# Dynamic convolution, layer norm and feed-forward on one core: the softmax by logarithms into two small PSUM tiles, another opening and another order of all engines

## The chip, the cores and the metric

The kernel runs on one core of one Trainium2 chip. The metric is device microseconds of one execution; before the change the median of three timed runs is 874.82 us (874.36 to 877.87). PE is TensorE, DVE is VectorE, ACT is ScalarE, POOL is GpSimd, and SP is the engine that issues most transfers.

## The reference

Inputs are x (8 x 4224 x 192, f32), weight_gen (8 x 4224 x 8 heads x 7), a layer-norm gain and two weights in f64 (192 x 768 and 768 x 192).

```python
w = softmax(weight_gen, axis=-1)                 # 7 taps, 1e-9 added to the sum
y[b, s, h*24+g] = sum_k w[b, s, h, k] * x_pad[b, s+k, h*24+g]   # 6 zero rows ahead
xn = (y - mean) / sqrt(var + 1e-6) * g_ln        # over the 192 columns
out = y + relu(xn @ w_ch1) @ w_ch2
```

## The kernel before, in words

The 33792 rows are laid out as 128 partitions x 264 columns of rows. A column holds one row of 192 values on every partition. Columns are taken in parts (`PARTS`: six of 4, six of 8, fifteen of 12, then 8 and 4) for the norm, in softmax pieces (`SOFT`: 4, 8, then 12 each) and in chunks of 4 or 6 columns for the convolution. x lies in a ring of 36 columns.

Softmax of a piece (L419 to L465): DVE takes the maximum (L434), POOL subtracts it (L436), ACT takes exp (L439), DVE sums (L443), ACT forms 1/sum as exp(-ln) (L446, L447), DVE refines it by three small instructions (L453 to L455), and DVE multiplies (L459) into one PSUM tile `wn` of two banks, which holds a whole piece.

Convolution of a chunk (L470 to L540): four DVE products (L505), `c0`, `c1`, `c3` with two taps each and `c2` with one tap into `y`; POOL issues two adding transfers (`d0`, `d1`, L511) and does four additions (`a0` to `a3`, L508). A part's norm (L548 to L647): ACT sums and squares row by row (L558, L563), a root by ln and exp (L586 to L588), five small DVE instructions (L591 to L597, "newton"), then for each group of 4 columns ACT scales (L609, `xh`) and rounds to f16 (L629, `hi`), POOL forms the low half (L642, `lo`), and SP issues a transposing transfer (L646, `turn`).

The feed-forward of a group has three units on PE (L664, 36 f16 products each, two row halves side by side) into one of two PSUM tiles `ph`; after each, ACT evicts with relu (L679) and DVE forms the low half (L681). The output is made in two halves, `p0` and `p1` (L715, 72 products each); the halves swap PSUM banks, so `p1` waits for an empty marker instruction, `hop`, that waits for `p0`; before the change the marker stands on SP (L725). DVE adds y (L767, `f`) and SP stores. The order on PE is unit, unit, p0 of the group before, unit, p1. 66 groups follow one another; the last output is L744.

The weights come as f64 and are rebuilt from their words in the opening (`from_double`, L810): ACT squares, four DVE steps put the words together, ACT sums squares; PE adds over partitions (L854), which gives a scale; ACT makes the high f16 half of W1 (L896), POOL the low one (L899), SP swaps partition halves (L903). W2 follows in the same manner (L919 to L933). Eleven products of 512 columns (L636, "wake") run on PE ahead of the first unit.

Every operation has a number in the table `PLACE`; operations are issued in the order of these numbers, so the table is the order on every engine. Engines take their own instructions strictly in that order. A `turn` and an adding transfer are also kept apart: each waits for the last of the other kind ahead of it.

Of the kernel before, what the change touches and what calls it, by code (L numbers as in the profile page):

```python
# [16 lines left out]
P = 128  # L17
ALPHA = 8.0
NT = 4

PARTS = (4,) * 6 + (8,) * 6 + (12,) * 15 + (8, 4)
SOFT = (4, 8) + (12,) * 21
DIRECT = 0
CHUNK = 6
RING = 36
# [6 lines left out]
    'wload': (0, 1, 30, 25, 35, 80, 81, 249, 257, 427, 634, 489, 783, 994, 748, 993, 1166, 1074, 1355, 1499,  # L32
        1370, 1571, 1769),
    'load': (6, 5, 33, 37, 36, 78, 79, 178, 183, 177, 256, 191, 340, 248, 303, 381, 426, 341, 568, 608, 564,
        713, 681, 682, 750, 780, 861, 953, 998, 1109, 997, 1176, 1157, 1235, 1263, 1368, 1289, 1460, 1531, 1572,
        1656, 1637, 1702, 1673, 1720, 1789, 1858, 1894, 1953, 2010, 2084, 2085),
    'w_load': (38, 24, 23, 7, 9, 10),
    'w_load2': (39,),
    'w_as': (82,),
    'w_av': (60, 62, 70, 89),  # L40
    'w_an': (100,),
    'w_cs': (102,),
    'w_cv': (26, 32, 48, 103),
    'w_cn': (105,),
    'w_s1': (120, 121, 123, 131, 139),
    'w_h': (154, 155, 145, 146),
    'w_l': (184, 152),
    'w_m': (189, 190, 182, 181),
    'w_c2s': (106, 122, 156),
    'w_c2v': (71, 85, 87, 115, 126, 128, 130, 132, 141, 143, 158, 161),  # L50
# [4 lines left out]
    'sub': (3, 8, 44, 51, 111, 237, 321, 432, 550, 665, 852, 758, 956, 1145, 1041, 1266, 1339, 1473, 1559, 1678,
        1757, 1855, 1970),
    'exp': (11, 16, 45, 52, 135, 277, 322, 440, 551, 666, 856, 802, 965, 1169, 1051, 1283, 1340, 1476, 1561,
        1695, 1784, 1869, 2005),
    'sum': (12, 17, 49, 53, 159, 279, 352, 456, 558, 687, 876, 832, 974, 1187, 1066, 1395, 1393, 1509, 1593,
        1716, 1802, 1875, 2024),  # L60
    'rcp': (13, 18, 54, 55, 160, 299, 437, 464, 640, 728, 882, 902, 986, 1192, 1172, 1399, 1446, 1510, 1594,
        1751, 1803, 1882, 2032),
# [34 lines left out]
    'sums': (64, 66, 95, 96, 136, 134, 170, 171, 239, 231, 247, 276, 318, 298, 320, 330, 395, 368, 392, 394,  # L97
# [163 lines left out]
def kernel(  # L261
# [735 lines left out]
```

## Time and profile before

| what | us |
|---|---|
| median of three timed runs | 874.82 |
| span of the profiled execution | 871.6 |
| PE, DVE, POOL, ACT busy | 793.9, 778.0, 697.6, 679.1 |
| first unit on PE starts | 67.02 |
| last product on PE ends | 867.26 |

The profiled execution's time is given by its span, from the first to the last instruction; the timed runs hold 3.2 us more around it. Busy is the time in which an engine worked; the two row halves of a unit run side by side, so a PE that is busy all the time is not yet a proof of a bound, which is why the chain and the gaps between products are read as well.

### The profile page before, as it was taken

The page shows a single profiled execution, that of the slowest core. Times are in us where ns is not written, and L with a number is a line of the kernel's source. Part 1 is how long each engine was busy: PE and PEld are TensorE (multiplying, and loading weights), DVE is VectorE, ACT ScalarE, POOL GpSimd, SP SyncE. Part 2 cuts the span into 40 slices and gives each one's busy share as a digit, 9 for nine tenths or more (in the row PEclk, how much of TensorE's full clock was granted, in tenths as well). Part 3 has the DMA queues.
Part 4 walks back from the last instruction along what each step waited for, and adds up shares of the span by engine and source line. Part 5 has one row for each costly group of instructions (what it writes and reads, how often), then busy time and mean ns, then how long its engine had stood idle before and what let it go on. Part 6 is the DMA issues. An engine that isn't in the chain of part 4 may idle for free.

```text
span 871.6 us, 37255 instructions
## 1 busy us (share of the span) xinstructions
PE 793.9 (91%) x16581; PEld 785.1 (90%) x16581; DVE 778.0 (89%) x799; ACT 679.1 (78%) x1776; POOL 697.6 (80%) x405
## 2 busy tenths in 40 slices
PE   0028999999999999999899999999999999999998
PEld 0016999999999999999899999999999999999997
DVE  6999999999999999999889999999999998974442
ACT  1798888888788898789598878787898888685741
POOL 4999999999789898897887988779888887857100
PEclk9999999999999999999999999999999999999999
DMA  8958878798897789789796798877988848643262
GB/s 210 270 119 182 181 161 179 143 190 191 185 199 149 169 183 216 137 179 180 152 212 142 156 210 163 164 200 178 182 167 157 205 111 196 117 84 77 44 178 56
DMA packets 138328, 143.23 MB, mean 164 GB/s; under 512 B 107575, under 2 KB 109111, under 8 KB 138167
## 3 DMA queue, kind: packets, MB, share of 16 engines
q1 hardware_dynamic: 123175, 88.95, 44.2%
q0 software_dynamic: 14688, 51.91, 31.0%
q8 instruction: 129, 2.11, 1.0%
q14 instruction: 32, 0.26, 0.1%
q10 hardware_dynamic: 304, 0.00, 0.0%
HBM read 36.43 MB, written 25.95 MB: 72 GB/s over the span
## 4 chain that ended last, share of the span: by engine, by line
PE 64%; ACT 1%; DVE 1%; issue 1%; DVEq 0%; ACTq 0%
PE po L715 32%; PE ph L664 32%; PE ph L744 1%; ACT junk L563 1%; DVE pr L505 1%; DVE hlo L681 0%; ACT junk L558 0%; ACT hh L679 0%; DVE y L767 0%; ACT s L586 0%; ACT rr L447 0%; ACT rr L446 0%; ACT s L587 0%; DVE wn L593 0%; DVE wn L595 0%
## 5 line engine op out<-in xcount | busy, mean ns | idle before, releaser
L508 POOL TENSOR_TENSOR y<-y,pr 128x1152 f32<-128x1152 f32 (+1 forms) x204 | 503.1, 2488 | 27.6 <-DMA pr<-pr 14.1
L664 PE MATMUL ph<-xT,c_w 64*128 64x256 f16 x7128 | 416.0, 270 | 8.9 <-DVE hlo L681 8.1
L664 PEld LDWEIGHTS <-c_w 64*128 64x128 f16 x7128 | 386.5, 94 | 14.0 <-issue 12.7
L715 PE MATMUL po<-c_w2h,hh 64*128 64x192 f16 x3120 | 388.1, 243 | 2.6 <-issue 2.5
L715 PE MATMUL po<-c_w2h,hlo 64*128 64x192 f16 x3120 | 388.1, 243 | 1.4 <-issue 1.4
L715 PE MATMUL po<-c_w2l,hh 64*128 64x192 f16 x3120 | 388.0, 243 | 0.5 <-issue 0.5
L505 DVE TENSOR_TENSOR pr<-x,wn 128x2304 f32<-128x2304 f32 (+1 forms) x153 | 337.2, 2214 | 3.8 <-DMA x<-in_x_dram 2.7
L715 PEld LDWEIGHTS <-hh 64*128 64x128 f16 x6240 | 309.4, 94 | 3.7 <-issue 3.7
L681 DVE SCALAR_TENSOR_TENSOR hlo<-ph,hh 128x1024 f16<-128x1024 f32 x198 | 238.6, 1217 | 52.3 <-ACT hh L679 52.0
L679 ACT ACTIVATE hh<-ph 128x1024 f16<-128x1024 f32 x198 | 199.5, 1014 | 108.0 <-PE ph L664 104.9
L715 PEld LDWEIGHTS <-hlo 64*128 64x128 f16 x3120 | 177.3, 94 | 1.5 <-issue 1.5
L642 POOL TENSOR_TENSOR hl<-xh,hl 128x768 f16<-128x768 f32 x66 | 113.8, 1758 | 52.1 <-ACT hl L629 52.1
L511 POOL DMA_DIRECT2D pr<-pr x102 | 102.2, 1110 | 53.7 <-DMA xT<-hl 33.2
L609 ACT ACTIVATE xh<-y,s 128x192 f32<-128x192 f32 x264 | 124.4, 535 | 18.7 <-DVE s L597 18.2
L563 ACT ACTIVATE junk<-y,s 128x192 f32<-128x192 f32 x264 | 119.6, 453 | 6.8
L558 ACT ACTIVATE junk<-y 128x192 f32<-128x192 f32 x264 | 95.0, 360 | 17.7 <-POOL y L508 11.6
L767 DVE SCALAR_TENSOR_TENSOR y<-po,c_fs,y 128x768 f32<-128x768 f32 (+1 forms) x80 | 68.0, 860 | 8.3 <-PE po L715 8.2
L505 DVE TENSOR_TENSOR y<-x,wn 128x1152 f32<-128x1152 f32 (+1 forms) x51 | 60.1, 1180 | 0.2
L854 PE MATMUL po<-c_s,ones 128*128 128x1 f32 x10 | 2.5, 356 | 59.9 <-DVE hlo L840 59.9
L854 PEld LDWEIGHTS po<-c_s,ones 128*128 128x128 f32 x10 | 2.3, 324 | 60.0 <-DVE hlo L840 60.0
L629 ACT ACTIVATE hl<-xh 128x768 f16<-128x768 f32 x66 | 54.5, 836 | 0.9
L558 ACT ACTIVATION_READ_ACCUMULATOR junk<-y 128x1 f32 x264 | 49.5, 188 | 0.0
(69 smaller groups left out, 312.1 us busy)
## 6 DMA issues: line engine op xcount, KB each, us to landing
pr<-pr POOLq DMA_DIRECT2D x60, 576.0 KB, 7.8
x<-in_x_dram SPq DMA_DIRECT2D x30, 576.0 KB, 6.5
out_dram<-y SPq DMA_DIRECT2D x30, 576.0 KB, 5.8
pr<-pr POOLq DMA_DIRECT2D x42, 384.0 KB, 5.9
x<-in_x_dram SPq DMA_DIRECT2D x20, 384.0 KB, 6.1
out_dram<-y SPq DMA_DIRECT2D x20, 384.0 KB, 4.2
w<-in_weight_gen_dram SPq DMA_DIRECT2D x21, 336.0 KB, 5.8
pr<-in_moe_w_ch_dram SPq DMA_DIRECT2D x1, 1152.0 KB, 19.1
```

The source lines that it names most:

```text
L505: E.tensor_tensor(out=ov, in0=xv, in1=wv, op=ALU.mult)
L508: Q.tensor_tensor(out=flat(0), in0=flat(0), in1=flat(k), op=ALU.add)
L511: return Q.dma_start(flat(to), flat(k), accum_op=ALU.add, max_dma_last_dim=CHUNK * D * 4)
L558: A.activation(junk, at(y)[:, j, :], AF.Identity, scale=-1.0 / D, accum_out=at(s4)[:, 3, t : t + 1])
L563: A.activation(junk, at(y)[:, j, :], AF.Square, bias=at(s4)[:, 3, t : t + 1], accum_out=at(s4)[:, 0, t : t + 1])
L609: A.activation(paired(xh, t), at(y)[:, i, :].rearrange("p (c q) -> p c q", q=P // 2), AF.Identity, bias=at(s4)[:, 3, g + t : g + t + 1], s ...
L642: lambda xh=xh, hl=hl: Q.tensor_tensor(out=halves(hl, True), in0=pairs(xh), in1=halves(hl, False), op=ALU.subtract),
L664: T_.matmul(ph[:, r, v * 2 * P : (v + 1) * 2 * P], W["w1"][rows, WB[r][c], w, f : f + P], xv[rows, a, c, :, :], start=(v == 0 and k == 0), ...
L679: lambda: A.activation(at(hh)[:, us, :], at(ph), AF.Relu), [ph], [(hh, u)])
L681: lambda: V.scalar_tensor_tensor(out=at(hlo)[:, us, :], in0=at(ph), scalar=0.0, in1=at(hh)[:, us, :], op0=ALU.max, op1=ALU.subtract),
L715: made.append(T_.matmul(at(po)[:, z, e * D : (e + 1) * D], token(b, 2 * z + e, j)[rows], W[w][rows, j, :], start=(ph == 0 and e == 0 and k ...
L767: V.scalar_tensor_tensor(out=ysl, in0=at(po)[:, zs[0] : zs[-1] + 1, : 2 * D], scalar=W["fs"][:, 0:1], in1=ysl, op0=ALU.mult, op1=ALU.add)
```

## The change

- Softmax: ACT writes exp into the weights' own tile; the sum's logarithm (ACT, `log`) is subtracted on POOL (`less`), and ACT takes exp of the difference chunk by chunk (`expw`) into one of two PSUM tiles `wn` of one bank. DVE's three refining instructions and its product L459 go.
- Parts: 4, 4, 4, then twenty of 12, then 8 and 4. The first part is cut into chunks of 2 columns.
- The first three chunks are summed on PE: 14 f32 products with the identity (`z0` to `z3`), ACT copies the sum to `y`. They have no adding transfers and no POOL additions. Of the first two chunks POOL does the fourth product.
- Weights: DVE has three steps in place of four (POOL does one small step); the low half of W1 is made on PE (a diagonal f32 product less an f16 one) and copied by ACT; W2's words are held in the x ring. The wake products go.
- The marker `hop` stands on ACT.
- All numbers of `PLACE` are new.

```diff
-PARTS = (4,) * 6 + (8,) * 6 + (12,) * 15 + (8, 4)
+PARTS = (4, 4, 4, 12, 12, ... 12, 8, 4)
+FIRST = 2
+ZPOOL = (0, 0, 0)
+PMUL = 2
 PLACE = {
-    'wload': (0, 1, 30, 25, 35, 80, 81, 249, ...
+    'wload': (2, 3, 16, 62, 23, ...
...
-    pool("wn", 1, [P, 2 * HALF], F32, pp)
+    pool("wn", 2, [P, HALF], F32, pp)
...
-        step("ACT", 2 * a_ns(m, 180), "rcp", ln, [sm], [rr])
-        step("V", 290 + 4.2 * m, "inv", newton, [sm, rr], ["ps"])
-        step("V", v_ns(m * K), "mul", ...
+        step("ACT", a_ns(m, 180), "log",
+             lambda: A.activation(at(sm)[:, :m], at(sm)[:, :m], AF.Ln, bias=bias[:, 1:2]), [sm], [sm])
+        step("Pool", 100 + 1.82 * m * K, "less",
+             lambda: Q.tensor_tensor(out=at(e)[:, :m], in0=at(e)[:, :m], in1=wide(sm), op=ALU.subtract), [sm, e], [e])
...
+        op("ACT", a_ns(n * HK), ("expw", t0),
+           lambda: A.activation(at(wn)[:, : n * HK], at(e)[:, o * H : (o + n) * H, :].rearrange("p m k -> p (m k)"), AF.Exp),
+           [e], [wn])
...
+        if c < len(ZPOOL):
+            z, h, by = Buf("ph"), nd // 2, ZPOOL[c]
             def gather(ks, first, last):
                 for k in ks:
                     for b in range(2):
                         T_.matmul(at(z)[:, b, :h], ident, flat(k)[:, b * h : (b + 1) * h],
                                   start=(first and k == ks[0]), stop=(last and k == ks[-1]))
...
-                op("PE", 4700, ("wake", 0), wake, [(hl, 0)], [wb], lat=0.0)
...
-            h = gp["hop"] = SY.nop()
+            h = gp["hop"] = A.nop()
...
-            op("SP", 60, ("hop", s), hop, [(po, 0)], [(po, "hop")])
+            op("ACT", 60, ("hop", s), hop, [(po, 0)], [(po, "hop")])
...
+                    T_.matmul(at(z)[:, b, :h], diag(i), src()[:, q], start=True, stop=False)
+                    T_.matmul(at(z)[:, b, :h], minus, hi()[:, q], start=False, stop=True)
```

What the table moves is shown at three places. The first is the head of PE's queue, before the first unit (L664); `c_s` are the partial sums of squares of the weights, `hl` the halves of the first group. Before:

```order
L854 MATMUL po_107<-c_s_122,ones 128x1 x2
L854 MATMUL po_107<-c_s_123,ones 128x1 x3
L636 LDWEIGHTS hl_83
L636 MATMUL ph_106<-hl_83 128x512
L664 LDWEIGHTS c_w_127
L664 MATMUL ph_105<-xT_86,c_w_127 128x256
```

And after, from the gather of the third chunk on (the two chunks ahead of it have four such rows each with 192 columns):

```order
L532 MATMUL ph_104<-pr_77,ident 128x384 x4
L532 MATMUL ph_104<-y_69,ident 128x384 x2
L532 MATMUL ph_104<-pr_76,ident 128x384 x4
L532 MATMUL ph_104<-pr_80,ident 128x384 x4
L855 MATMUL po_106<-c_s_123,ones 128x1 x2
L913 MATMUL ph_105<-hlo_90,xh_81 128x384
L914 LDWEIGHTS minus
L914 MATMUL ph_105<-c_w_128,minus 128x384
L855 MATMUL po_106<-c_s_124,ones 128x1 x3
```

The weights' sum now stands behind all gathers of the three chunks, and the low halves of W1 stand between the two sums.

The second place is the opening of DVE, from the first product on. Before (`hh_88` holds words of W1):

```order
L505 TENSOR_TENSOR pr_76<-x,wn_104 128x2x768
L505 TENSOR_TENSOR pr_77<-x,wn_104 128x2x768
L505 TENSOR_TENSOR y_67<-x,wn_104 128x768
L505 TENSOR_TENSOR pr_78<-x,wn_104 128x2x768
L830 TENSOR_SCALAR ph_105<-hh_88 128x384
L453 TENSOR_SCALAR wn_104<-sm_97 128x64
L454 TENSOR_TENSOR wn_104<-wn_104,rr_95 128x64
L455 SCALAR_TENSOR_TENSOR wn_104<-wn_104,rr_95 128x64
```

And after, up to the first two words' steps (L835 to L841 are the old L830 to L836):

```order
L507 TENSOR_TENSOR y_69<-x,wn_103 128x768
L454 TENSOR_REDUCE sm_94<-w_64 128x96
L507 TENSOR_TENSOR pr_80<-x,wn_103 128x2x768
L449 TENSOR_REDUCE mx_93<-w_65 128x96
L507 TENSOR_TENSOR y_70<-x,wn_103 128x1152
L507 TENSOR_TENSOR pr_78<-x,wn_103 128x2304
L507 TENSOR_TENSOR pr_79<-x,wn_103 128x2304
L835 TENSOR_SCALAR ph_105<-xh_82 128x384
L838 SCALAR_TENSOR_TENSOR ph_105<-hh_89,ph_105 128x384
L841 SCALAR_TENSOR_TENSOR hlo_90<-hh_89,ph_105 128x384
```

W1's steps come behind the three first chunks and three products of a 6-column chunk, and then in one piece.

The third place is SP's queue where W1's halves are swapped (`c_w`) and the first groups are turned (`xT`). Before:

```order
L416 DMA w_66<-in_weight_gen_dram 128x1x672
L410 DMA x<-in_x_dram 128x1x768 x2
L646 DMA_TRANSPOSE xT_85<-hl_84 128x12x128
L646 DMA_TRANSPOSE xT_86<-hl_83 128x12x128
L903 DMA c_w_127<-c_w_127 64x2x384 x2
L410 DMA x<-in_x_dram 128x1x768
L903 DMA c_w_127<-c_w_127 64x1536 x2
```

And after:

```order
L431 DMA w_64<-in_weight_gen_dram 128x1x672
L425 DMA x<-in_x_dram 128x1x1152 x3
L922 DMA c_w_128<-c_w_128 64x1536 x2
L922 DMA c_w_128<-c_w_128 64x2x384 x2
L646 DMA_TRANSPOSE xT_85<-hl_83 128x12x128
L646 DMA_TRANSPOSE xT_86<-hl_84 128x12x128
```

The first group's turn now stands behind the four swaps on the same queue.

## Rows read from the trace of the kernel before

**Rows 1.** The core: its span in us and TensorE's mean granted clock.

```profile
core 0: 871.6 us, clock 0.997
```

**Rows 2.** The chain that ended last: start, us, what.

```profile
441.55 2.97 PE po L715 x72
444.52 3.93 PE ph L664 x72
...
861.20 6.06 PE ph L744 x72
867.28 0.62 DVE y L767
```

**Rows 3.** Timeline of PE: start, us, operation, count, idle before it.

```profile
48.50 1.01 PE L854 MATMUL po<-c_s,ones 128*128 128x1 f32 x4 [48.50 <-DVE hlo L840]
60.93 1.44 PE L854 MATMUL po<-c_s,ones 128*128 128x1 f32 x6 [11.41 <-DVE hlo L840]
62.23 4.85 PE L636 MATMUL ph<-hl 128*128 128x512 f16 x11
67.02 4.53 PE L664 MATMUL ph<-xT,c_w 64*128 64x256 f16 x72
75.44 5.42 PE L664 MATMUL ph<-xT,c_w 64*128 64x256 f16 x72 [3.89 <-DVE hlo L681]
...
103.25 4.11 PE L664 MATMUL ph<-xT,c_w 64*128 64x256 f16 x72
```

**Rows 4.** Waits of PE: us in total, times, longest.

```profile
PE ph L664 <- DVE hlo L681: 8.1, 10, 3.9
PE po L715 <- issue: 4.4, 3, 2.5
```

**Rows 5.** Busy us (and count) of each engine in three stretches.

```profile
10.00:100.00 90.00, 35.68 (x557) 30.54 (x559) 86.49 (x121) 64.82 (x186) 82.48 (x56) 0.98 0.83 194
103.00:867.00 764.00, 754.93 (x15958) 751.57 (x15954) 684.96 (x663) 607.91 (x1577) 608.94 (x339) 1.00 0.76 161
400.00:600.00 200.00, 196.09 (x4180) 195.75 (x4176) 189.35 (x180) 164.07 (x431) 165.20 (x88) 1.00 0.85 182
```

**Rows 6.** Timeline of DVE in the opening.

```profile
10.74 3.42 DVE L505 TENSOR_TENSOR pr<-x,wn 128x1536 f32<-128x1536 f32 x2 [2.72 <-DMA x<-in_x_dram]
14.08 0.95 DVE L505 TENSOR_TENSOR y<-x,wn 128x768 f32<-128x768 f32 x1
...
34.58 0.15 DVE L591 TENSOR_SCALAR wn<-s 128x4 f32<-128x4 f32 x1
...
35.33 0.15 DVE L597 TENSOR_TENSOR s<-wn,s 128x4 f32<-128x4 f32 x1
```

**Rows 7.** Groups by shape: busy us, mean ns of one, idle before.

```profile
L681 DVE SCALAR_TENSOR_TENSOR hlo<-ph,hh 128x1024 f16<-128x1024 f32 x198 | 238.6, 1217 | 52.3 <-ACT hh L679 52.0
L505 DVE TENSOR_TENSOR pr<-x,wn 128x2304 f32<-128x2304 f32 x90 | 228.1, 2543 | 1.0 <-POOL y L508 0.7 <-DVE wn L455 0.2
L505 DVE TENSOR_TENSOR y<-x,wn 128x1152 f32<-128x1152 f32 x30 | 40.3, 1344 | 0.1
L436 POOL TENSOR_TENSOR e<-w,mx 128x672 f32<-128x672 f32 x21 | 33.0, 1572 | 0.0
L459 DVE TENSOR_TENSOR wn<-e,wn 128x672 f32<-128x672 f32 x21 | 18.0, 857 | 0.4
L434 DVE TENSOR_REDUCE mx<-w 128x96 f32<-128x672 f32 x21 | 17.7, 842 | 0.0
L439 ACT ACTIVATE e<-e 128x672 f32<-128x672 f32 x21 | 15.8, 753 | 15.6 <-POOL e L436 15.6
L453 DVE TENSOR_SCALAR wn<-sm 128x96 f32<-128x96 f32 x21 | 5.3, 254 | 0.3
```

**Rows 8.** Transfers: count, size, median us from issue to landing.

```profile
pr<-pr POOLq DMA_DIRECT2D x60, 576.0 KB, 7.8
xT<-hl SPq DMA_TRANSPOSE x66, 3.6
```

More of the change, by code (lines that the diff above doesn't have):

```diff
@@ L31 @@
 PLACE = {
[L32 to L38, printed above, removed]
@@ L55 @@
[L55 to L62, printed above, removed]
@@ new lines @@
+    'w_load': (34, 36, 40, 85, 0, 1),
+    'w_load2': (61,),
+    'w_as': (73,),
+    'w_ap': (74,),
+    'w_av': (91, 93, 96),
+    'w_an': (98,),
+    'w_cs': (79,),
+    'w_cp': (80,),
+    'w_cv': (83, 86, 87),
+    'w_cn': (88,),
+    'w_s1': (103, 108, 123, 125, 128),
+    'w_d': (147, 142),
+    'w_h': (130, 141),
+    'w_l': (149, 143),
+    'w_lc': (160, 148),
+    'w_m': (168, 166, 170, 169),
+    'w_c2s': (99, 101, 102),
+    'w_c2p': (100, 112, 111),
+    'w_c2v': (110, 114, 116, 126, 131, 132, 118, 120, 122),
@@ new lines @@
+    'newton': (105, 162, 224, 272, 365, 463, 558, 655, 759, 869, 984, 1078, 1177, 1285, 1391, 1480, 1582, 1680,
[16 rows of a table added]
+    'turn': (178, 189, 243, 295, 334, 338, 408, 418, 427, 499, 492, 570, 581, 627, 621, 707, 708, 735, 791, 835,
[21 rows of a table added]
+    'halo': (184, 517, 711, 966, 1276, 1593, 2005),
+    'unit': (192, 198, 213, 218, 226, 238, 257, 269, 286, 309, 319, 331, 350, 352, 366, 383, 387, 401, 416, 423,
[10 rows of a table added]
+    'relu': (203, 206, 219, 225, 234, 246, 270, 293, 300, 317, 320, 335, 353, 369, 374, 388, 393, 406, 428, 429,
[10 rows of a table added]
@@ L193 @@
+    'hlo': (207, 212, 222, 227, 242, 256, 275, 303, 308, 328, 329, 342, 357, 375, 376, 397, 395, 413, 431, 433, 448,
[14 rows of a table added]
+    'hop': (240, 292, 325, 372, 402, 442, 474, 512, 546, 575, 614, 653, 686, 718, 753, 785, 821, 855, 892, 925, 959,
[16 rows of a table added]
 }
@@ L457, in softmax @@
-        step("V", 290 + 4.2 * m, "inv", newton, [sm, rr], ["ps"])
-        step("V", v_ns(m * K), "mul",
-             lambda: V.tensor_tensor(out=WN[:, : m * K].rearrange("p (m k) -> p m k", k=K),
-                                     in0=at(e)[:, :m], in1=wide(ps), op=ALU.mult),
-             [e, "ps"], ["wn"])
-        pa["e"] = e
-        if S0 < sum(ch["n"] for ch in chunks[:DIRECT]):
-            step("ACT", a_ns(m * K), "keep",
-                 lambda: A.copy(at(e)[:, :m].rearrange("p m k -> p (m k)"), WN[:, : m * K]), ["wn"], [(e, "w")])
@@ L467, in at_pair @@
-    def at_pair(b, n):
-        return lambda: at(b)[:, :, :n, :].rearrange("p k t d -> p k (t d)")
+             lambda: Q.tensor_tensor(out=at(e)[:, :m], in0=a3(wb), in1=wide(mx), op=ALU.subtract), [wb, mx], [e])
+        step("ACT", a_ns(m * K), "exp", lambda: A.activation(a3(wb), at(e)[:, :m], AF.Exp), [e], [wb])
+        step("V", v_ns(m * K), "sum",
+             lambda: V.tensor_reduce(out=at(sm)[:, :m], in_=a3(wb), axis=AX.X, op=ALU.add), [wb], [sm])
+        step("ACT", a_ns(m, 180), "log",
+             lambda: A.activation(at(sm)[:, :m], at(sm)[:, :m], AF.Ln, bias=bias[:, 1:2]), [sm], [sm])
@@ L527, in gather @@
                                   start=(first and k == ks[0]), stop=(last and k == ks[-1]))
[L529 to L530 removed]
+            for i in range(by):
+                op("Pool", q_ns(nd), (f"a{i}", t0), lambda k=6 - i: add(k), [(prs[5], 1 - i)], yw)
+            rest = tuple(range(5, 7 - by))
+            sums = ((1, 2), (3, 4), rest, (0,)) if by else ((1, 2), (0,), (3, 4), rest)
+            sums = [ks for ks in sums if ks]
+            for i, ks in enumerate(sums):
+                op("PE", nd * len(ks) / 0.6, (f"z{i}", t0),
+                   lambda ks=ks, i=i: gather(ks, i == 0, i == len(sums) - 1),
                    [q for k in ks for q in ([(prs[(k - 1) // 2 * 2 + 1], (k - 1) % 2)] if k else yw)], [z], lat=400.0)
             op("ACT", a_ns(nd, 150), ("copy", t0),
[L533 removed]
+               lambda: A.copy(at(y)[:, :n, :].rearrange("p (b t) d -> p b t d", b=2),
+                              at(z)[:, :, :h].rearrange("p b (t d) -> p b t d", d=D)), [z], yw)
             return
@@ L590, in newton @@
         def newton():
-            V.tensor_scalar(out=aux(0), in0=row(0), scalar1=1.0 / (D * A2 * A2), scalar2=1e-6 / (A2 * A2),
-                            op0=ALU.mult, op1=ALU.add)
+            V.tensor_scalar(out=aux(0), in0=row(0), scalar1=EPS, scalar2=None, op0=ALU.add)
             V.tensor_tensor(out=aux(1), in0=aux(0), in1=row(2), op=ALU.mult)
@@ L807, in load_weights, with from_double @@
         dma("SP", SY, "load2", lambda: words(2, 0, 2 * NF * D).rearrange("p (j d) -> p j d", d=2 * D), wv2,
-            8 * NF * D, raw[2])
-    def from_double(want, src, dst, n, sq, r, w, space="ph", rows=slice(0, P), scale=1.0, more=()):
-        m, t = Buf("pr"), Buf(space)
+            8 * NF * D, *(xkey(t) for t in range(late, RING)))
+    def from_double(want, src, dst, n, sq, r, w, space="ph", rows=slice(0, P), scale=1.0, more=(), hold="xh"):
+        m, t = Buf(hold), Buf(space)
         def part(i):
@@ L824, in tv @@
             return a[rows].bitcast(dt)[:, :n]
-        squared, want, normed = ((f"w_{want}{p}", 0) for p in "svn")
-        op("ACT", a_ns(n), squared, lambda: A.activation(mv(), part(1).bitcast(F32), AF.Square), r, [m])
+        squared, kept, want, normed = ((f"w_{want}{p}", 0) for p in "spvn")
+        op("ACT", a_ns(n), squared, lambda: A.activation(mv(), part(1).bitcast(F32), AF.Abs), r, [m])
+        op("Pool", 100 + 1.2 * n, kept,
+           lambda: Q.tensor_scalar(out=mv(), in0=mv(), scalar1=TINY, scalar2=None, op0=ALU.max), [m], [m])
         op("V", v_ns(n), want,
-           lambda: V.tensor_scalar(out=tv(I32), in0=part(1), scalar1=3, scalar2=0x3FFFFFFF,
-                                   op0=ALU.logical_shift_left, op1=ALU.bitwise_and), r, [t])
+           lambda: V.tensor_scalar(out=tv(I32), in0=mv().bitcast(I32), scalar1=3, scalar2=0x3FFFFFFF,
+                                   op0=ALU.logical_shift_left, op1=ALU.bitwise_and), [m], [t])
         op("V", v_ns(n), want,
@@ L917, in weights @@
             from_double("c2", lambda h=h: words(2, 2 * h * tn, 2 * tn), lambda h=h: f32(w2r, tn, h * tn),
-                        tn, s2[:, h : h + 1], [raw[2]], [(w2r, h)], "po")
+                        tn, s2[:, h : h + 1], [xkey(t) for t in range(late, RING)], [(w2r, h)], "po", hold="pr")
         want2 = ("w_s2", 0)
```

231 lines of the change are left out of this document (122 added, 109 removed), and 214 rows, old and new, of the table PLACE.

## The prediction

> **What bounds the kernel now.** I read the span, then the chain that ended last, then PE's own timeline and waits, and last what the other engines do beside it.
>
> The chain [rows 2] is PE from the opening to the end: a unit takes 1.96 us, half an output 2.97, the last output 6.06, and 867.28 starts the last DVE work. A group of four columns so takes 3 x 1.96 + 2 x 2.97 = 11.8 us. All of PE's work is 198 units x 1.964 (two in 3.93) + 130 halves x 2.97 + 6.06 = 781 us. The first unit starts at 67.02 [rows 3], the last product ends at about 867.3, so 800.3 - 781 = 19 us are lost in between. The time is: first unit + 781 + losses + 4.3 of tail. The change leaves the 781 and the tail alone; it can act on the opening and on the losses only.
>
> Where are the losses? I cut at the fourth group, column 12, whose units start at 103.25 [rows 3]. Ahead of them PE does nine units and four halves, 29.6 us, and has had 103.25 - 67.02 = 36.2: 6.6 lost, 3.89 of them in one wait for DVE's hlo. Behind it 751.5 us of work take 764.0: 12.5 lost. The waits of PE [rows 4] name 8.1 us for hlo, of which 3.89 are the one above, the 0.4 before the next unit is small beside it, and I put 3.8 behind column 12; 4.4 are "issue", in which PE waited for nothing that is shown; the rest is in small pieces. The window from 103 to 867 [rows 5] says the same: PE is idle for 9.1 us of 764.
>
> DVE is what PE waits for. In the opening it is busy 86.5 of 90 us [rows 5], and from 400 to 600 us 94.7% (189.35 of 200), when ACT and POOL have 82%. So I take DVE's queue as the clock of the opening.
>
> **The change part by part.** All sums are made against the profiled execution, 871.6 us [rows 1]; the timed median, 874.82, is 3.2 us more, which I add at the end.
>
> *The opening.* DVE's first product stood at 10.74 after 2.72 us of waiting for x [rows 6]. The first piece of x is now smaller (two columns and half of the six leading ones), and what stands ahead of it is exp of a small piece on ACT; I start DVE at 10.74 - 2.72 = 8.0. DVE instructions follow each other closely: two of 1.75 us in 3.42, and the next at 14.08, 0.08 before the pair ended. I use durations less 0.08. What DVE has ahead of column 12's first unit, from the order:
> - products: two chunks of 2 columns, 2 x (2 x 0.87 + 0.47) = 4.4 (0.87 from the y product of 14.08 with as many elements, 0.47 by proportion); two of 4 columns, 2 x (3 x 1.67 + 0.87) = 11.8; four of 6 columns, 4 x (3 x 2.46 + 1.26) = 34.6, and three products of a fifth, 6.2 [rows 7]: 57.0;
> - ten maxima and sums, 0.76 each: 7.6; four norm steps, 0.90 each (34.58 to 35.48, [rows 6]): 3.6;
> - the weights' words: 12 steps of 384 and 3 of 768 elements at the same 0.47 and 0.87, and small ones: 9.6;
> - nine hlo at 1.14: 10.3; three merges, about 2.
>
> Together 90.1, so 98.1 without any wait. DVE idled for 3.5 of 90 us in the same stretch before [rows 5]; I take the same: column 12 starts at 101.6 against 103.25, **1.7 us earlier**. Bounds: DVE without idle time, 98.1 (5.2 earlier); and x and exp no earlier than before, with the idle time doubled, 108 (4.5 later).
>
> Hidden in this: 4 norm columns wait for less than a 12-column part does. Column 12's norm needs all sums to column 23, so the lead of the first unit cannot all survive. I put the first unit at 58: W1's last words leave DVE after 23.5 us of its queue (4.4 + 5.9 + 6.2 of products, the rest maxima, sums and words), at 31.5, and the sum on PE follows at 32.6; before, the sum at 48.50 was 18.5 us ahead of the first unit [rows 3]; I add 7 because four swaps now stand ahead of the turn on SP (the turn lands 3.6 us after its issue, [rows 8]) and because ACT has norm work between. That is 9 us earlier than 67.02, and PE then waits in the groups 1 to 3 for ACT's relu, which has all of W2's scaling ahead of it, and for DVE.
>
> *Wake products removed.* They are 512 columns in 0.44 us (62.23, eleven in 4.85), the lower of the two clock levels, 1.2 GHz; the 72 products behind them take 4.53 us, those of 75.44, after a wait, 5.42, against 3.93 at 2.4 GHz [rows 2, 3]. Without the wake the first units cost at most 3.9 us more. It is covered: ACT's first relu comes later than the second unit. I take 0, bounds 0 and 3.9.
>
> *Gathers on PE.* 28 f32 products of 192 columns and 14 of 384; the table sets W1's sum behind them, so they must be over by 32.6. The trace has f32 products of one column only: six rows for three products in 1.44 us [rows 3], two rows each, 0.24 a row, which is the load of 128 weights. Lower bound: 0.24 per row with 192 columns, 0.32 with 384 (columns at 1.2 GHz beside the load): 56 x 0.24 + 28 x 0.32 = 22.4 us. Upper bound: each value costs two column times, as the weights do, and nothing is beside the load: 56 x 0.56 + 28 x 0.88 = 56 us. With two column times beside the load it is 56 x 0.32 + 28 x 0.64 = 35.8 at 1.2 GHz and about 22 at 2.4 GHz. I take a value between these two, nearer to the second, 24 us. The first product of DVE ends at 8.0 + 0.9 = 8.9, so the gathers end at 33, about in time. At the lower level throughout 44.7, 12 late; at the upper bound 65, 32 late.
>
> The Trainium skill, page "FP8 and Floating Point Precision", section "TensorE Precision Notes", says that true FP32 takes four passes through the array. The trace shows two rows for a product and cannot tell how many column times each has. By the rule, four column times for each of 10752 columns are 35.8 us at 1.2 GHz: the third of the values above.
>
> *The softmax on DVE.* Per 12 columns L459 (0.78 net) and three small ones (0.25 each) go: 1.6 us. From 400 to 600 DVE has 189.35 us, 33.6 per 35.5 us of PE (three groups); 32.0 remain, 90%. POOL gets one more subtraction, 1.57 [rows 7], on 29.3: 30.9, 87%. ACT gets one more exp in two pieces, about 0.95 by L439, and the marker, on 29.1: 30.1, 85%. No engine reaches PE. DVE's margin doubles, and at column 12 it has done more convolution (to column 39 in place of 35, by the order). I take the 3.8 us of hlo waits behind column 12 as gone: **-3.8**. Bounds: all 12.5 gone, or none. The "issue" waits stay; PE's instructions are as many as before.
>
> *Marker on ACT.* `hop` must come between p0 and p1, with one unit, 1.96 us, to hide it. On ACT it stands behind relu, exp and norm work, and ACT behind it waits for p0. In the trace it cannot be seen. I take 0; bounds 0 and 2.97 in each of 65 groups.
>
> *Low halves of W1* leave POOL and go to PE and ACT in the opening; they are in the 7 us above. Transfers: 14 adding ones fewer (7.8 us each to land, [rows 8]), which opens nothing on the path.
>
> Sum: 871.6 - 1.7 - 3.8 = 866.1; with 3.2 outside, **869.3 us**.
>
> The Trainium skill, page "PSUM — Partial Sum Buffer", section "Engine vs sequencer instructions", says that an empty instruction waits only until those ahead are dispatched, not until they end. No row here shows it. By that rule the marker passes ahead of ACT's running work, and its price stays near 0, as taken.
>
> **Rivals.**
> - *The lead is kept.* If column 12 is not held up by DVE (98.1 or earlier, with a norm that follows at once), 5 to 9 us of the first unit's lead remain: 874.8 - 8.5 - 3.8 = 862.5. For it: DVE has its words of W1 done at 31.5 and only 90 us of work. Against it: ACT, POOL and DVE come out within a few us of each other at column 12.
> - *Gathers at the lower clock.* PE's products stay at 1.2 GHz because PE has pauses for its inputs; W1's sum is 12 us late, some 2 are taken up by later waits: 874.8 + 10 - 3.8 = 881. It decides from about 38 us for the end of the gathers on. For it: the clock was at its lower level in the whole opening before. Against it: from 9 us on the queue of gathers is dense.
> - *The marker on ACT.* 0.15 us late in each of 65 groups is +9.8: 879. It decides where ACT lags PE by more than 1.6 us at the marker; its idle share of 18% speaks against it, its strict order for it.
> - *No gain.* The small waits behind column 12 are not DVE's load but single products of 2.5 us ahead of an hlo, which stay: 873.1.
>
> **How the numbers follow.** What one measurement of this kernel can tell from no change is about 0.5%, 4.4 us: faster is under 870.4, slower over 879.2. Forecast 0.45 (864 to 874: 0.28 faster, 0.17 same); lead kept 0.20 (faster); gathers 0.15 (slower); marker 0.10 (half same, half slower); no gain 0.10 (0.02 faster, 0.08 same). Sum: faster 0.50, same 0.30, slower 0.20. The range 857 to 881 takes in the kept lead and the nearer of the slow cases.
>
> **What would show it.** Right: the first unit at 55 to 61; column 12's units at 99 to 104 with a PE wait ahead of them; hardly a wait for hlo behind it; DVE near 90% from 400 to 600. The gathers are right if their rows end by 33 and W1's sum follows at once; wrong if the sum waits for them. The marker is wrong if pieces of idle time stand ahead of L715 in most groups. The whole is wrong if column 12 comes after 108, or if PE waits for POOL or ACT in the middle for more than 5 us.

## The result, and the profile after

The changed kernel takes 882.51 us (median of 9 runs, 878.08 to 885.95) against 874.61 of the kernel before (9 runs): ratio 1.0092 with a 95% interval of 1.0068 to 1.0115. It is slower by 0.9%; 869.3, faster by 0.6%, had been forecast, and the range ended at 881. In a later series of both kernels it stood at 1.0043 (1.0017 to 1.007; 881.40 against 876.49). So 8 us by the first series, 5 by the second, were lost where 5.5 were to be won.

The span and the granted clock, against [rows 1]:

```profile
core 0: 882.2 us, clock 0.976
```

PE's timeline, against [rows 3] (start, us, operation, count, idle time ahead of it). First the last gather, the weights' sum and the first units, then column 12 and the place where most is lost:

```profile
24.59 5.32 PE L532 MATMUL ph<-pr,ident 128*128 128x384 f32 x16
33.93 1.01 PE L855 MATMUL po<-c_s,ones 128*128 128x1 f32 x4 [4.01 <-ACT xh L844]
...
59.39 6.43 PE L664 MATMUL ph<-xT,c_w 64*128 64x256 f16 x72 [6.94 <-DMA xT<-hl]
68.14 4.11 PE L664 MATMUL ph<-xT,c_w 64*128 64x256 f16 x72 [2.32 <-DVE hlo L681]
...
100.50 4.13 PE L664 MATMUL ph<-xT,c_w 64*128 64x256 f16 x72 [0.25 <-DMA xT<-hl]
...
785.98 6.65 PE L664 MATMUL ph<-xT,c_w 64*128 64x256 f16 x72 [4.05 <-DMA xT<-hl]
```

The opening has come out: the first unit at 59.39 (before 67.02), column 12 at 100.50 (before 103.25). So 2.75 us are won by column 12, and all that is lost is lost behind it: from column 12 to the last product the kernel before needed 764.0 us, this one needs 777.1.

The busy times in the stretches of [rows 5]:

```profile
10.00:100.00 90.00, 59.58 (x711) 49.41 (x711) 86.45 (x94) 70.59 (x200) 81.53 (x49) 0.83 0.83 187
103.00:867.00 764.00, 747.98 (x15738) 732.82 (x15735) 644.49 (x560) 611.50 (x1578) 615.91 (x332) 0.99 0.76 160
400.00:600.00 200.00, 197.25 (x4173) 191.67 (x4170) 181.63 (x158) 169.02 (x443) 174.89 (x95) 1.00 0.83 176
```

From 400 to 600 us DVE is busy for 181.63 us (90.8%, before 94.7%), POOL for 87.4%, ACT for 84.5%. No engine beside PE is full, and still PE does less in the same time.

The waits of PE behind column 12, against [rows 4] (us in all, times, longest):

```profile
PE po L715 <- issue: 5.4, 6, 1.9
PE ph L664 <- DMA xT<-hl: 4.7, 2, 4.1
PE ph L664 <- issue: 2.2, 4, 0.7
PE ph L664 <- DVE hlo L681: 1.6, 3, 0.9
PE po L715 <- DVE y L767: 1.4, 1, 1.4
PE po L715 <- ACTq L725: 0.4, 1, 0.4
```

The waits for hlo have become few. New is a wait for a turn of 4.1 us and a wait of p0 for the sum `f` (L767) of the group before. "Issue" is 7.6 us in all, where this profile of the kernel before has 5.0 and three further ones 4.0, 7.0 and 7.7, so it is not clearly more.

The chain of waits around the long one (start, us, what):

```profile
773.03 3.20 POOL hl L642 x2
776.23 1.02 POOL y L510
777.24 8.69 DMA xT<-hl
785.93 0.04 issue
785.98 6.65 PE ph L664 x72
```

This is column 236. The table of numbers has, in this order (number, engine, operation, column):

```
2128 SP   turn 232      2181 POOL d1 256      2195 POOL lo 236
2162 POOL d0 252        2182 POOL d1 260      2196 SP   turn 240
2167 POOL d0 256        2194 POOL lo 240      2197 SP   store
                                              2198 SP   turn 236
```

The high half of column 236 was there at number 2171, but its low half and turn stand behind four adding transfers and behind the low half and the turn of column 240, which PE needs only a group later. The last adding transfer, `d1 260`, has landed at 772.95. POOL then makes the low half of 240 until 774.62 and that of 236 until 776.23. Turn 240 is issued at 774.65, a store next, and then turn 236 (SP's queue; start, us, what):

```profile
776.14 0.99 SPq L775 DMA_DIRECT2D out_dram<-y  x1
777.24 4.29 SPq L646 DMA_TRANSPOSE xT<-hl  x1
```

It lands at 785.93. Its issue takes 4.29 us and its landing 8.7, where other turns of this stretch take 1.4 and 4.2 to 4.5. PE comes for it at 781.7. With a landing of 4.4 us, that of turn 240 here, it would have been there at 781.6 (an estimate from these rows): the second place costs 2.6 us by the later start and 4.3 by the slow transfer. From 784.42, while PE still waits, the granted clock is at one half (1.2 GHz) for 6.8 us, and the two units take 6.65 us in place of 3.93.

A sum over all of PE's pauses behind column 12 shows what else there is. Each distance from one product's start to the next is taken less a fixed allowance (54.5 ns in a unit, 41.1 in a half, some 48 at a border), and put down to the place in which it lies (a "piece" is one unit or one half). The allowance cancels between the columns of this table; only differences count:

```
us behind column 12                  before   changed   one trade   three trades
profiles (mean of)                      3        2          1            1
unit behind a unit (hlo)               5.5      2.6        2.3          2.5
unit behind a half (mostly turn)       4.9     10.4        5.0          5.9
half behind a unit (f, marker)         5.9      8.3        7.6          6.0
packet end of the program              9.9     13.5       15.5         13.5
inside a piece (clock)               -11.0     -9.4       -8.0        -11.7
sum                                   15.2     25.4       22.4         16.1
```

The trades are experiments below. "Before" has the profile shown and two later ones, of 871.6, 875.0 and 872.1 us; a further one of 881.0 has a sum of 22.6. The changed kernel's two have 882.2 and 878.2. Its sum is 10.2 us larger, column 12 is 3.1 earlier (100.2 against 103.3): 7.1 in all, and the spans differ by 880.2 - 872.9 = 7.3. The account closes, and it has five entries: hlo -2.9, turn +5.4, the clock +1.6 (part of it behind the late turn, part behind another pause, at 303.63), p0's wait +2.4, the program +3.6. With the profile of 881.0 among those of before, hlo, turn and clock stay as they are, but p0's wait falls to +1.1 and the program to +2.9: these two lie within the spread of the profiles. The profile of the one trade is of an execution 4.0 us above the median of its runs, so the sum of its column is too large for a comparison of times.

### The profile page after: what moved, and what is told of

Its sections match the earlier page's. It is cut to its first block, busy times and chain, and to the rows that moved or that the text cites. A ratio compares the mean times of both kernels' runs of the same rounds, so it can differ in the third digit from the quotient of the medians.

```text
span 882.2 us, 37253 instructions
## 1 busy us (share of the span) xinstructions
PE 822.3 (93%) x16663; PEld 796.0 (90%) x16663; DVE 740.9 (84%) x670; ACT 690.1 (78%) x1796; POOL 704.4 (80%) x391
## 3 DMA queue, kind: packets, MB, share of 16 engines
q8 instruction: 130, 2.13, 1.0%
## 4 chain that ended last, share of the span: by engine, by line
PE 46%; POOL 30%; issue 8%; DMA 7%; DVE 5%; ACT 4%; SPq 0%; POOLq 0%; DVEq 0%; ACTq 0%
PE ph L664 23%; PE po L715 22%; POOL y L510 20%; POOL hl L642 4%; DMA xT<-hl 3%; POOL pr L513 3%; DVE pr L507 3%; DMA pr<-pr 3%; POOL e L451 1%; POOL e L458 1%; DVE hlo L681 1%; ACT junk L571 1%; ACT junk L576 1%; PE ph L744 1%; DMA x<-in_x_dram 1%
## 5 line engine op out<-in xcount | busy, mean ns | idle before, releaser
L510 POOL TENSOR_TENSOR y<-y,pr 128x1152 f32<-128x1152 f32 (+1 forms) x176 | 474.2, 2707 | 27.1 <-DVE y L507 13.1
L664 PE MATMUL ph<-xT,c_w 64*128 64x256 f16 x7128 | 419.4, 271 | 22.4 <-DMA xT<-hl 13.0
L664 PEld LDWEIGHTS <-c_w 64*128 64x128 f16 x7128 | 379.7, 95 | 38.8 <-DMA xT<-hl 15.0
L507 DVE TENSOR_TENSOR pr<-x,wn 128x2304 f32<-128x2304 f32 (+2 forms) x139 | 333.8, 2412 | 5.0 <-POOL y L510 2.9
L715 PEld LDWEIGHTS <-hh 64*128 64x128 f16 x6240 | 304.1, 94 | 9.9 <-issue 8.1
L715 PEld LDWEIGHTS <-hlo 64*128 64x128 f16 x3120 | 172.4, 94 | 2.0 <-issue 1.8
L513 POOL DMA_DIRECT2D pr<-pr x88 | 85.0, 1065 | 44.2 <-DMA xT<-hl 17.0
L767 DVE SCALAR_TENSOR_TENSOR y<-po,c_fs,y 128x768 f32<-128x768 f32 (+1 forms) x86 | 68.4, 813 | 5.0 <-PE po L715 4.6
L507 DVE TENSOR_TENSOR y<-x,wn 128x1152 f32<-128x1152 f32 (+2 forms) x47 | 59.6, 1267 | 1.7 <-ACT wn L470 1.7
L576 ACT ACTIVATION_READ_ACCUMULATOR junk<-y,s 128x1 f32 x264 | 49.4, 187 | 0.0
L451 POOL TENSOR_TENSOR e<-w,mx 128x672 f32<-128x672 f32 (+2 forms) x23 | 33.8, 1470 | 7.8 <-DVE mx L449 6.6
```

The costliest lines, as they stand in the source:

```text
L507: E.tensor_tensor(out=ov, in0=xv, in1=wv, op=ALU.mult)
L510: Q.tensor_tensor(out=flat(0), in0=flat(0), in1=flat(k), op=ALU.add)
L513: return Q.dma_start(flat(to), flat(k), accum_op=ALU.add, max_dma_last_dim=CHUNK * D * 4)
L576: A.activation(junk, at(y)[:, j, :], AF.Square, scale=SQ, bias=at(s4)[:, 3, t : t + 1], accum_out=at(s4)[:, 0, t : t + 1])
L664: T_.matmul(ph[:, r, v * 2 * P : (v + 1) * 2 * P], W["w1"][rows, WB[r][c], w, f : f + P], xv[rows, a, c, :, :], start=(v == 0 and k == 0), ...
L715: made.append(T_.matmul(at(po)[:, z, e * D : (e + 1) * D], token(b, 2 * z + e, j)[rows], W[w][rows, j, :], start=(ph == 0 and e == 0 and k ...
```

## The experiments

**The changed kernel again** (a_again), for a second profile.

> The changed kernel once more, for a second profile. Theory (late turn and late program): the wait of PE for the turn of column 236 near 782 us is there again (4 us, then a stretch at the lower clock), since it comes from the order; the pauses of PE in the middle of a piece fall on the same places in its program (matmuls 92 behind a multiple of 128) but not on the same pieces, 6 to 12 us in all. Rival (POOL is the bound): no single wait stands out twice, the losses lie in POOL's chain everywhere. Ratio to before about 1.009 by either.

881.40 us, ratio 1.0043 (1.0017 to 1.007). The turn is late again; this is its row among PE's waits:

```profile
PE ph L664 <- DMA xT<-hl: 5.1, 2, 4.5
```

The pauses within a piece are ten again, 9.6 us in all (9.7 in the first profile). Six of the ten lie at the same products as in the first profile (near 206, 344, 369, 482, 526 and 708 us there), four at others: the expectation, that they would fall on other pieces, holds for four only.

**One trade of places** (a_swap).

```diff
+_swap("lo", 59, 60)      # columns 236 and 240 change numbers
+_swap("turn", 59, 60)
```

> The changed kernel with the low half and the turn of column 236 ahead of those of column 240. Theory (late turn): the wait at 782 us and the slow stretch behind it go, 4.25 + 2.6 = 6.8 us, so about 876 (ratio 1.001). Rival (POOL's added subtraction is the bound): POOL has the same work, so PE waits elsewhere a little later and no more than 2 us are won (ratio 1.007 to 1.009).

875.66 us beside the 881.40 of the changed kernel in the same series: 5.7 us faster, ratio to the kernel before 0.9986 (0.9963 to 1.0009). POOL has the same work. PE's waits behind column 12 (the lines of the kernel are 10 higher):

```profile
PE po L725 <- issue: 6.3, 6, 2.2
PE ph L674 <- issue: 3.4, 4, 1.4
PE po L725 <- DVE y L777: 2.0, 1, 2.0
PE ph L674 <- DVE hlo L691: 1.1, 2, 0.9
PE ph L674 <- DMA xT<-hl: 0.7, 1, 0.7
```

SP's queue at these two turns (now 236 first, then 240):

```profile
776.74 1.59 SPq L656 DMA_TRANSPOSE xT<-hl  x1
778.43 0.65 SPq L785 DMA_DIRECT2D out_dram<-y  x1
779.20 4.29 SPq L656 DMA_TRANSPOSE xT<-hl  x1
```

The slow second turn is still there (8.6 us to landing), but it is now that of 240, which has time; turn 236 lands 4.2 us after its issue, and PE comes for it at 783.8. Two pairs of numbers in a table make the loss of this series. POOL's load doesn't. Low half and turn were traded together, so their shares are not shown apart.

**The marker back on SP** (a_hop_sp).

```diff
-            h = gp["hop"] = A.nop()
+            h = gp["hop"] = SY.nop()
-            op("ACT", 60, ("hop", s), hop, [(po, 0)], [(po, "hop")])
+            op("SP", 60, ("hop", s), hop, [(po, 0)], [(po, "hop")])
```

> The changed kernel with the marker back on SP. Theory: PE waited only 0.4 us for the marker on ACT, so at most 1 us faster; SP waits for p0 again ahead of turns and stores, so it may be slower by up to 4. Rival (the marker on ACT costs 0.15 us a group, as in the prediction): 9.8 us faster, ratio 0.998.

882.94 us, ratio 1.0068 (1.0038 to 1.0098): no gain. On SP the marker makes PE wait, and on ACT it doesn't:

```profile
PE po L715 <- SPq L725: 8.0, 5, 3.0
...
PE ph L664 <- DMA xT<-hl: 0.2, 1, 0.2
```

The marker stands on SP behind the slow issue of a turn here (779.04, 4.02 us), and held up p1 ahead of column 236 by 3.2 us, where the turn had cost 4.3; so one took the place of the other.

**POOL's second subtraction left out for the most part** (a_less8).

```diff
-  Q.tensor_tensor(out=at(e)[:, :m], in0=at(e)[:, :m], in1=wide(sm), op=ALU.subtract)
+  Q.tensor_tensor(out=at(e)[:, :8], in0=at(e)[:, :8], in1=wide(sm)[:, :8], op=ALU.subtract)
```

> The changed kernel with the second subtraction on POOL cut to 8 of 96 sums (the other weights stay undivided): POOL has 1.3 us less in every 12 columns, some 26 us in all. Theory (late turn by its place, program fetched late): the turn of column 236 still stands behind that of 240 and four adding transfers that wait for DVE's products; 0 to 2 us faster, ratio 1.002 to 1.008 to the kernel before. Rival (POOL's added work is the bound): all of the loss goes, ratio 0.998 or lower.

881.38 us, ratio 1.0059 (1.0034 to 1.0084): as the changed kernel. 26 us less on POOL buy nothing, though the chain of waits runs over POOL for 30% of the span, and the wait for the turn of 236 is still 4.5 us. Here the chain through POOL told that POOL's place in the order is on the path, not that its load is.

**The maximum and the sum of each 12-column piece twice on DVE** (a_dve2).

```diff
+            if n == 12:
+                V.tensor_reduce(out=at(o)[:, :m], in_=a3(wb), axis=AX.X, op=alu)
             return V.tensor_reduce(out=at(o)[:, :m], in_=a3(wb), axis=AX.X, op=alu)
```

> The changed kernel with the maximum and the sum of every 12-column piece done twice on DVE: 1.5 us more in every 12 columns, about what the change took from DVE. The prediction's term (DVE's load makes the waits for hlo): 3.8 us slower than the changed kernel, ratio 1.009 to 1.013. Rival (DVE has room, the losses lie elsewhere): within 1 us of it, ratio 1.004 to 1.009 as in its own runs.

895.62 us (four runs), ratio 1.0215 (1.0177 to 1.0254). The changed kernel stands at 1.0043 to 1.0092 in other series, so this is 11 to 15 us slower. Both expectations missed; DVE is nearer to the bound than either said. Column 12, in PE's timeline:

```profile
106.56 2.67 PE L668 MATMUL ph<-xT,c_w 64*128 64x256 f16 x44 [0.89 <-DVE hlo L685]
```

It starts 6.1 us later than in the changed kernel. Ten doubled reductions stand ahead of it, 10 x 0.76 = 7.6 us of DVE: in the opening DVE's queue passes on 0.8 of what is added. Behind column 12 the waits for hlo rise from 1.6 to 7.2 us:

```profile
PE ph L668 <- DVE hlo L685: 7.2, 10, 0.9
```

**The kernel before with less softmax on DVE** (b_light). The three small instructions and the product L459 work on 8 of 96 sums.

```diff
+        m8 = m if S0 < 36 else 8
-            V.tensor_scalar(out=ps, in0=at(sm)[:, :m], ...
+            V.tensor_scalar(out=ps, in0=at(sm)[:, :m8], ...
-  WN[:, : m * K] ... in0=at(e)[:, :m], in1=wide(ps), op=ALU.mult
+  WN[:, : m8 * K] ... in0=at(e)[:, :m8], in1=..., op=ALU.mult
```

> The kernel before with the division of the softmax on DVE cut to 8 of 96 sums in the pieces from column 36 on (the other weights keep the values of an earlier piece), so DVE has some 1.1 to 1.3 us less in every 12 columns. The prediction's term (waits for hlo are DVE's load): 3 to 4 us faster, ratio 0.996. Rival (these waits are single long products ahead of an hlo, and the order stands as it is): 0 to 1 us, ratio 0.999 to 1.001.

872.46 us, ratio 0.9964 (0.9936 to 0.9992): 3.2 us faster by the ratio, with an interval of 0.7 to 5.6. That is the size which the prediction took for DVE's load, but the interval reaches into the rival's 0 to 1. The waits for hlo behind column 12, first in the kernel before (b_again3; other profiles have 3.8 to 4.7), then in this run:

```profile
PE ph L664 <- DVE hlo L681: 3.8, 7, 1.1
PE ph L666 <- DVE hlo L683: 2.2, 4, 1.4
```

So the one profile shows 2 of the 3.2 us as fewer waits for hlo.

**Three trades of places** (a_best): the first one; the same for columns 144 and 148 (the turn of 144 makes PE wait for 0.9 us near 505 us); and the maximum of piece 180 behind `f` of column 96 and an hlo. Of the last, this is DVE with one trade only (start, us, operation, idle time ahead):

```profile
369.82 1.21 DVE L691 SCALAR_TENSOR_TENSOR hlo<-ph,hh 128x1024 f16<-128x1024 f32 x1
374.08 0.85 DVE L459 TENSOR_REDUCE mx<-w 128x96 f32<-128x672 f32 x1 [3.05 <-POOL e L461]
374.85 1.01 DVE L777 SCALAR_TENSOR_TENSOR y<-po,c_fs,y 128x768 f32<-128x768 f32 x1
```

The maximum waits 3.05 us for its buffer, which POOL still reads, and `f` and an hlo behind it on DVE wait too, and with them p0.

```diff
+_trade(("lo", 36), ("lo", 37))
+_trade(("turn", 36), ("turn", 37))
+_trade(("hlo", 75), ("f", 31), ("max", 16))
```

> The changed kernel with three trades of places: low half and turn of column 236 ahead of those of 240, of 144 ahead of 148, and on DVE the maximum of piece 180 behind the sum f of column 96 and an hlo. Theory (waits made by single places in the order): 5.7 us as in the first trade, 0.9 us of the wait at 505 us and 2 us of the wait at 372 us: 8 to 9 us faster than the changed kernel, 872 to 874 where the kernel before has 876, ratio 0.995 to 0.997. Rival (what is won at one place is lost at the next): as with the first trade alone, 0.9986.

874.15 us (the kernel before in this series: 876.03), ratio 0.9997 (0.9971 to 1.0023). The wait for `f` is gone, and of the waits for a turn 0.8 us are left, as with one trade:

```profile
PE po L730 <- issue: 6.3, 7, 1.5
PE ph L679 <- issue: 1.4, 2, 0.9
PE ph L679 <- DVE hlo L696: 1.1, 2, 0.9
PE ph L679 <- DMA xT<-hl: 0.8, 2, 0.4
```

What the other two trades brought beyond the first can't be told from the times: the theory's 0.995 to 0.997 did not come, and the rival's 0.9986 lies inside the interval.

**Where PE's program comes late.** "Issue" in the middle of a half can't be a wait for data. The trace has the packets that bring PE's program ("q8 instruction: 130" in the page's table of queues, 2.13 MB, so 16 KB or 128 products with their weight loads each). With all products numbered, every pause of over 0.3 us inside a piece lies behind product 92 modulo 128 in the changed kernel, 94 in the kernel before, and ends 1.2 to 1.6 us after a packet has landed. Four of them (the pause counted from one product's start to the next):

```
kernel    pause at   us     product    modulo 128   packet from - to
before    422.07     2.78    7262          94        422.41 - 423.37
before    526.54     1.62    9438          94        525.85 - 526.73
changed   303.63     2.19    4956          92        303.47 - 304.41
changed   708.11     1.07   13276          92        706.88 - 707.80
```

Most packets start within 3 us of the moment at which PE enters the packet ahead; these four start 4.5 to 6.5 us after it. In the 2 us from that moment adding transfers kept 14 or more of the 16 queues busy; at other such pauses (206, 319, 369 and 482 us in the changed kernel) it was loads and stores. All fifteen pauses of the two profiles have full queues (15.5 or more) in these 2 us, but so have 107 of the other crossings from packet to packet, which cost no such pause: every late packet here met full queues, but full queues do not always make one late. Three groups of runs tested this.

*Adding transfers of half the size* in the changed kernel (a_halfadd):

```diff
-            return Q.dma_start(flat(to), flat(k), accum_op=ALU.add, ...
+            return Q.dma_start(flat(to)[:, : nd // 2], flat(k)[:, : nd // 2], accum_op=ALU.add, ...
```

> The changed kernel with the adding transfers of POOL cut to the first half of their columns (the other half of these sums is left out), so 288 KB in place of 576. Theory (PE's program comes late when a transfer that fills all 16 queues stands ahead of it): of the ten pauses in the middle of a piece the five or six behind adding transfers go, those behind loads and stores of x stay: 4 to 5 us; the turn of column 236 still stands behind the same transfers, but they land some 2 us earlier: together 5 to 8 us faster, ratio 1.000 to 1.003. Rival (POOL's own work is the bound): its additions are as long as before, 0 to 2 us.

876.52 us, 4.9 less than the changed kernel in the same series, ratio 1.0001 (0.9978 to 1.0023). "Issue" is down from 7.6 us to 2.9, with seven pauses, 4.5 us in all, in place of ten, 9.7 in all. The late turn is as late as before, though the adding transfers land sooner: the last one ahead of it is there at 765.03, and turn 240 is issued at 767.70, when its low half is done. So the turns wait for POOL's low halves, not for the transfers:

```profile
PE ph L664 <- DMA xT<-hl: 5.0, 2, 4.1
PE ph L664 <- DVE hlo L681: 3.5, 4, 2.0
PE ph L664 <- issue: 2.0, 3, 1.1
PE po L715 <- DVE y L767: 1.8, 1, 1.8
PE po L715 <- issue: 0.9, 3, 0.4
```

*Empty products* (a_best_s32, a_best_s64, a_best_s96): 32, 64 or 96 products of one column in a stretch of the opening in which PE waits shift all that follows in PE's program.

```diff
+                for _ in range(32 if not W.get("shift") else 0):
+                    T_.matmul(at(z)[:, 1, 400:401], minus, minus[:, :1], start=True, stop=True)
+                W["shift"] = True
```

> As the three trades, with 32 empty products of one column (64 instructions) in PE's queue in a stretch of the opening in which PE waits: all that follows stands 32 products later in PE's program. Theory (pauses in the middle of a piece are the program coming late): they stay, but lie 32 products later modulo 128 (124 in place of 92), and meet other transfers, so their sum may be anything from 5 to 13 us. Rival (they come from the work itself): the same pieces pause, ratio as without the 32.

> As before with 64 empty products. Theory: pauses at 28 modulo 128; their sum changes again, 5 to 13 us. Rival: the same pieces pause, the same ratio.

> As before with 96 empty products. Theory: pauses at 60 modulo 128; the sum changes again, 5 to 13 us. Rival: the same pieces pause, the same ratio.

871.59 us, ratio 0.9969 (0.9942 to 0.9996); 876.11, ratio 1.0005 (0.9974 to 1.0036); 876.32, ratio 1.001 (0.9984 to 1.0036). The expectations counted the shift the wrong way round: counted with the empty products, the pauses stay at product 93 modulo 128; counted without them, they fall 32, 64 and 96 products earlier in the work. They belong to the packets of the program and not to the pieces. Their sums are 8.7, 8.1 and 11.9 us. The first of the three is the only complete version that was measured faster than the kernel before; its interval ends just under 1, and it is one of three that differ in nothing but the shift.

*The same halves in both kernels* (b_halfadd: the kernel before, a_best_half: the three trades), with two more profiles of the kernel before (b_again2, b_again3; another, b_again, is the one of 881.0).

> The kernel before with its adding transfers cut to half of their columns (the other half of these sums is left out). Theory (the changed kernel loses more to its program coming late): the pauses in the middle of a piece fall from some 6 us to 3, so 2 to 3 us faster here, ratio 0.997, less than the 5 us that the changed kernel won. Rival (both lose the same): 5 us, ratio 0.994.

> The three trades with the adding transfers cut to half (the other half of these sums is left out). Theory: pauses in the middle of a piece fall from some 10 us to 4 or 5, so 5 us faster than the three trades, ratio 0.992 to 0.994 to the kernel before as it is. Rival (the halves helped only the late turn, which is gone): 0 to 2 us, ratio 0.996 to 0.998.

> The kernel before once more, for a second profile. Theory (PE's program comes late where a long transfer has all queues): its pauses in the middle of a piece lie again one packet of its program (128 products) or a multiple of it apart, but at other pieces; 4 to 8 us in all behind column 12, against 10 to 12 in the three profiles of the changed kernel. Rival (the same in both kernels, only the one profile differed): 9 to 12 us here too.

> A third profile of the kernel before. Theory: pauses in the middle of a piece 4 to 8 us in all behind column 12, against 8 to 12 in eight profiles of the changed kernel and its trades. Rival: 8 to 12 here too.

> A fourth profile of the kernel before, for the same: 4 to 8 us by the theory, 8 to 12 by the rival.

Both come to 0.9946 of the kernel before (0.9928 to 0.9964 and 0.9927 to 0.9964), so both win 0.5%. The pauses of four profiles of the kernel before sum to 6.0, 9.4, 8.4 and 5.5 us, those of the two profiles of the changed kernel to 9.7 and 9.6, of the one trade and the three to 11.8 and 9.9; with halved transfers 3.1 are left in the kernel before and 2.6 in the three trades. So the rival in b_halfadd, that both kernels lose the same, came out in the times, and two of the three repeats of the kernel before lie above the theory's 4 to 8 us. Three kernels win 4 to 5 us by halved transfers, and their pauses shrink by 4 to 7; that all of the win is the program is not shown, since halved transfers also leave the queues free for turns, loads and stores. That a late program costs the changed kernel 2 to 4 us more than the kernel before is what some profiles say and what the times don't confirm. This stays open.

## Why the prediction was wrong, step by step

*The opening: right.* Column 12 was put at 101.6 and came at 100.5 and 99.9; the first unit at 58, it came at 59.4. The steps between came as taken, too: W1's last words left DVE at 32.8 (31.5 taken), the sum on PE followed at 33.93 (32.6), and the first unit waited 6.94 us for its turn, which SP issued at 55.94 behind the four swaps. That DVE's queue is its clock is borne out by the doubled reductions. The lead of the first unit shrinks from 7.6 us to 2.75 by column 12, as said.

*Gathers: right.* They end at 24.59 + 5.32 = 29.9 (33 were taken) and take 20.8 us of PE (24 were taken). Behind 13 us a row takes 0.17 us with 192 columns and 0.33 with 384 at a granted clock of 1.0, so two column times at 2.4 GHz, and a product has two rows: four column times a product, the third of the prediction's values at the upper clock. W1's sum stands idle ahead of 33.93 for ACT, not for them. The rival of the slow gathers is out.

*Wake products: right.* The first two units take 6.43 us in place of 4.53, and the next still waits 2.32 us for hlo, so the slower clock (granted 0.5 until 64.21) was covered.

*Marker on ACT: right.* 0.4 us in all, and moving it back won nothing.

*Loads of the engines: right.* 90, 87 and 85% were worked out; 90.8, 87.4 and 84.5% were measured.

*The 3.2 us added at the end: right in the sum, wrong in its reason.* The timed executions hold 1.8 us more than their span (884.04 against 882.2), not 3.2; by that, the other 1.4 is that the profiled execution was quicker than the median.

*Waits for hlo behind column 12: about right in size, wrong as the whole of what happens there.* They fell by 2.9 us (3.8 taken), and b_light won 3.2 (0.7 to 5.6) in the old order.

*The step that failed* is the sentence behind it: "Bounds: all 12.5 gone, or none." It lets the losses behind column 12 only shrink, and puts the new order of the turns there at nothing without a reason. All numbers of the table are new there as well, and I had followed the order through the opening alone and treated the turns, low halves and adding transfers of the 63 groups behind it by the engines' loads alone. In that stretch the table has eight places where a turn stands ahead of that of an earlier column. Seven of them cost 0.9 us or nothing, since their low halves are done 8 to 14 us ahead of their units. The eighth, column 236, has 5.5 us from its low half to the moment at which PE comes for it; it costs up to 7 us by the account and 5.7 by the trade. An inversion alone is no sign of a loss: the table before has six, and behind column 12 its profile shows no wait for a turn. A mean load can't show which one costs; the order could have, by what POOL has ahead of the low half and what SP has ahead of the turn. The signs of being wrong named a wait of PE for POOL or ACT in general, the rivals ACT's marker; none named a turn.

The wait of p0 (1.1 to 2.4 us) is of the same kind: one maximum whose buffer POOL still holds, with `f` queued behind it. The "issue" term was noted ("4.4 are 'issue'") and left unchanged because PE's instructions are as many as before; the profiles have the program's entry 2.9 to 3.6 us larger, unconfirmed. The Trainium skill, page "Runtime: NRT & Kernel Launch", section "Instruction fetch mechanics", says that a program is refilled in blocks of 16 KiB and that crossing one is mostly hidden. The size agrees with the packets here, and of 125 crossings behind column 12 in the changed kernel 115 cost no pause of over 0.3 us inside a piece; the other ten, where long transfers stand ahead, cost 9.7 us, and over all profiles of complete versions single pauses reach 3.1 us and an execution loses 5 to 12.

Of the 13 us between 869.3 and 882.5, the late turn is 5.7 by the trade and 6 to 7 by the account; the wait for `f`, 1 to 2, and the program, up to 4, are argued from the profiles and not shown by the times. The opening and hlo came as taken within 1.5.

## What to carry to other kernels

Where an order is rewritten, look at each place at which two operations of the same kind change their sequence, and ask for the one that is needed first: what stands ahead of it on its queue, when is that done, and how long before its use is it ready. Most inversions cost little or nothing, here seven of eight. Loads by engine, however well worked out, bound only the mean; one inverted pair can cost more than all that was won. And before a wait is put down as "issue", see whether it lies where the program itself is fetched.

## What had not been expected of the hardware

- PE stops in the middle of a half where a packet of its program comes late, and the packet is late where long transfers have the queues: pauses of 0.3 to 3.1 us, 5 to 10 in an execution of a complete version.
- Behind the pause at column 236 (4.3 to 4.8 us) the granted clock was at its lower level for 6.8 us in one profile and for 3.4 in four others; behind a pause of 2.19 us (at 303.63 in the changed kernel) for 3.4; behind one of 2.78 us in the kernel before (at 422) not at all.
- A turn that is issued right behind a store, which is itself right behind another turn, takes 3.8 to 4.5 us to issue and 6.7 to 8.7 to land (five such turns in each of the profiles after, a_again and a_swap); with 5 us of quiet ahead of it on its queue the median is 1.4 and 3.4 to 3.8.
- A row of an f32 product of 192 columns took 0.32 to 0.34 us up to 12.6 us and 0.16 to 0.18 from there to 18.8; one of 384 columns took 0.33. The clock's records start at 13.01, with the upper level until 33.49.
